# Attention ahead of two feed-forward layers: a pair's products with the values in two lumps instead of five parts

## The chip, the cores and the metric

The kernel runs on one core of a Trainium2 chip. The metric is the device time of one execution in microseconds (us). TensorE (PE) multiplies matrices, VectorE (DVE) and ScalarE (ACT) read its results, GpSimd (POOL) does small work beside them, and SyncE (SP) issues transfers.

## The reference

```python
def _attn_ref(q, k, v, tau):                      # 4 x 8 heads, 576 rows, 64 columns, float32
    scores = scale * np.matmul(q, k.transpose(0, 1, 3, 2))
    thresh = np.max(scores, axis=-1, keepdims=True) - tau
    scores = np.where(scores >= thresh, scores, -1000000000.0)
    scores = scores - np.max(scores, axis=-1, keepdims=True)
    attn = np.exp(scores)
    attn = attn / (np.sum(attn, axis=-1, keepdims=True) + 1e-09)
    return np.matmul(attn, v).astype(np.float32)

def reference(...):
    x = attn_out.transpose(0, 2, 1, 3).reshape(B * S, H * D)      # 2304 x 512
    x = _moe_ref(x, ...)      # sigmoid(x @ w_gate) * (x @ w_val) @ w_out, inner width 1536
    return _moe2_ref(x, ...)  # g(x @ w_in) @ w_out, inner width 2048
```

## The kernel before

The first quarter of the span is attention, the rest the two feed-forward layers. The change touches attention alone. It treats two heads at a time: 16 pairs `p`, each in five steps `u` = 0 to 4. Steps 0 to 3 take 128 rows of queries for both heads (`e` = 0, 1); step 4 takes the 64 rows that are left of each head together as one block of 128. The loop over `t` runs over all steps (`p, u = divmod(t, 5)`), and each turn of it issues work of several stages:

- `scores` (PE, L252, L248 in step 4): queries by keys of step t into `wa` (head 0) and `wb` (head 1);
- `turns` (PE, L295, L296): transposes of the weights of step t-2 into `wt` and `left`;
- `attend` (PE, L319): transposed weights by values into `av`. A round 0 takes the 256 rows of steps 0 and 1, a round 1 the 320 rows of steps 2 to 4; each has five blocks of 128 keys, and each block two matmuls, one a head. The table `rounds` says at which step, counted from the pair's first, which blocks of which round are done;
- `maxima` (DVE, L261): scaling out of `wa` and `wb` into an `s` of two buffers, with the row's extreme;
- `copies` (ACT, L301, L305): `wt` and `left` of step t-2 into `r`, `rl`;
- `exponents` (ACT, L273) of step t;
- `drain` (ACT, L329): `av` into `xall`, where a round ends;
- `masks` (DVE, L281): weights `p` of step t-1, then `lt` (POOL, L288), which `turns` needs for its last transpose;
- `background`: conversions of the feed-forward weights. In step 0 of pairs 1 to 12 three DVE operations (L155 to L169) stand between `maxima` and `masks`; in step 0 of pairs 13 to 15 splits of the first feed-forward operands stand there.

So each engine has a fixed order, written out by the loop: on PE scores of t, transposes of t-2, products with values; on DVE maxima of t, background, masks of t-1. Scores of t+1 overwrite what maxima of t read. A float32 matmul is two matmul instructions in the profile, a transpose one: a round of ten matmuls is 20 instructions there.

`load_v` loads a pair's values into one of three buffers `vs`, with four transfers on SP's queue, in step 4 two pairs ahead. SP's queue also carries queries and keys (`load`, step 2), the sums of a pair (`dr`, step 2 of the next pair) and their spread over partitions (`rb`, step 3).

Of the kernel before, what the change touches and what calls it, by code (L numbers as in the profile page):

```python
# [10 lines left out]
F32 = mybir.dt.float32  # L11
F32R = mybir.dt.float32r
U32 = mybir.dt.uint32
AF = mybir.ActivationFunctionType
# [15 lines left out]
def kernel(  # L30
# [17 lines left out]
    nc = tc.nc  # L48
# [3 lines left out]
    NP, _, S = q.shape  # L52
    D = v.shape[3]
# [4 lines left out]
    P = 128  # L58
    HS = S // 2
    nf, R = divmod(S, P)  # L60
# [48 lines left out]
    def run(*gens):  # L109
        for g in gens:  # L110
            for _ in g:
                pass
# [87 lines left out]
    def attention():  # L200
# [6 lines left out]
        left, av = (banks.tile([P, 512], F32, name=n) for n in ("left", "av"))  # L207
# [5 lines left out]
        per, pp = sb("per", 1), sb("pp", 2)  # L213
# [1 line left out]
        U = nf + 1  # L215
        N = NP * U
        NR = (2 * P, 2 * P + R)
        rt = [per.tile([P, 2, nf, n], F32, name=f"r_{i}") for i, n in enumerate(NR)]
        rl = [per.tile([P, n], F32, name=f"rl_{i}") for i, n in enumerate(NR)]
        vs = [per.tile([P, 2, nf + 1, D], F32, name=f"v_{i}") for i in range(3)]  # L220

        qk, st, pt, lts, drs = {}, {}, {}, {}, {}
# [7 lines left out]
        def load_v(p):  # L230

            t = vs[p % 3]
            for e in range(2):
                es = slice(e * R, e * R + R)
                nc.sync.dma_start(out=t[:, e, :nf], in_=v[p][:, e * (nf + 1) : e * (nf + 1) + nf])
                nc.sync.dma_start(out=t[es, e, nf], in_=v[p][es, nf])
# [6 lines left out]
        def scores(p, u):  # L243
            t = qk[p]
            for s in range(2):
                c = slice(s * HS, s * HS + HS)
                if u == nf:
                    nc.tensor.matmul(wa[:, s, :HS], corners[p % 2], t[:, 1, c], start=True, stop=True)  # L248
                    continue
                for e, w in enumerate((wa, wb)):  # L250
                    es = slice(e * D, e * D + D)
                    nc.tensor.matmul(  # L252
                        w[:, s, :HS], t[es, 0, u * P : u * P + P], t[es, 1, c], start=True, stop=True
                    )

        def maxima(p, u):

            t = sp.tile([P, 2, 2, HS], F32, tag="s", name="s")
            mx = mxs[(p * U + u) % 2]
            for e, w in enumerate((wa, wb)[: 1 if u == nf else 2]):  # L260
                nc.vector.tensor_scalar(  # L261
                    t[:, e], w[:, :, :HS], nscale, None, op0=ALU.mult, op1=ALU.min, accum_out=mx[:, 0, e : e + 1]
                )
                nc.gpsimd.tensor_scalar(
                    mx[:, 1, e : e + 1], mx[:, 0, e : e + 1], tau_b, None, op0=ALU.add
                )
            st[p, u] = t, mx

        def exponents(p, u):
            t, mx = st[p, u]  # L270
            ex = pe_.tile([P, 2, 2, HS], F32, tag="ex", name="ex")
            for e in range(1 if u == nf else 2):
                nc.scalar.activation(ex[:, e], t[:, e], AF.Exp, scale=-1.0, bias=mx[:, 0, e : e + 1])  # L273
            st[p, u] = t, mx, ex
# [15 lines left out]
        def turns(p, u):  # L290
            pr = pt.pop((p, u))
            for e in range(1 if u == nf else 2):
                for c in range(nf):
                    cs = slice(c * P, c * P + P)
                    nc.tensor.transpose(wt[:, e, cs], pr[:, e, cs], ident)  # L295
            nc.tensor.transpose(left[:, :P], lts.pop((p, u)).rearrange("p a b -> p (a b)"), ident)  # L296

        def copies(p, u):
            r, o = min(u // 2, 1), u % 2 * P if u < nf else 2 * P
            if u < nf:  # L300
                nc.scalar.activation(  # L301
                    rt[r].rearrange("p e c n -> p (e c) n")[:, :, o : o + P],
                    wt.rearrange("p e (c n) -> p (e c) n", n=P), AF.Copy,
                )
                nc.scalar.activation(rl[r][:, o : o + P], left[:, :P], AF.Copy)  # L305
                return
            for e in range(2):
                es = slice(e * R, e * R + R)
                x = wt[:, 0].rearrange("p (c n) -> p c n", n=P)
                nc.scalar.activation(rt[r][:, e, :, o : o + R], x[:, :, es], AF.Copy)  # L310
                nc.scalar.activation(rl[r][es, o : o + R], left[es, es], AF.Copy)

        def attend(p, r, cs):


            n = NR[r]
            for c in cs:
                for e in range(2):
                    nc.tensor.matmul(  # L319
                        av[e * D : e * D + D, :n], vs[p % 3][:, e, c], rt[r][:, e, c] if c < nf else rl[r],  # L320
                        start=c == 0, stop=c == nf,
                    )

# [4 lines left out]
        def drain(p, r):  # L328
            nc.scalar.activation(x_of(p)[:, r * NR[0] : r * NR[0] + NR[r]], av[:, : NR[r]], AF.Copy)  # L329

        def denom(p):
            rs = sums[p % 2]
            nc.vector.reciprocal(rs, rs)

        def sum_rows(p):

            n = 2 * nf + 1
            nc.scalar.activation(rows[p % 2][:n], left[:n, P : 2 * P], AF.Copy)
            drs[p] = dram.tile([n, P], F32, tag="dr", name="dr")
            nc.sync.dma_start(out=drs[p], in_=rows[p % 2][:n])  # L340
# [7 lines left out]
        def normalise(p, s):  # L348
            x, c = x_of(p), slice(s * HS, s * HS + HS)
            nc.gpsimd.tensor_tensor(x[:, c], x[:, c], rbs[:, p % 2 * S :][:, c], op=ALU.mult)  # L350
# [32 lines left out]
        corner(0)  # L383
        bg = background()

        rounds = {5: (0, 0, 2), 6: (0, 2, 5), 7: (1, 0, 2), 8: (1, 2, 4), 9: (1, 4, 5)}
        final = {5: (0, 0, 5), 7: (1, 0, 5)}
        parts = {}
        for p in range(NP):
            for i, (r, a, b) in (rounds if p + 1 < NP else final).items():  # L390
                parts.setdefault(p * U + i, []).append((p, r, range(a, b)))
        for t in range(N + 9):
            p, u = divmod(t, U)
            on = t < N
            mk = divmod(t - 1, U) if 1 <= t <= N else None
            at = divmod(t - 2, U) if 2 <= t <= N + 1 else None

            pd, ud = divmod(t - U, U)
            pd2, ud2 = divmod(t - 2 * U, U)
            if ud2 in (2, 3) and 0 <= pd2 < NP:  # L400
                normalise(pd2, ud2 - 2)
            if on:
                scores(p, u)
            if t == N + 1:
                yield t - N, True
            if at:
                turns(*at)
            if ud == 2 and 0 <= pd < NP:
                nc.tensor.transpose(left[: 2 * nf + 1, P : 2 * P], sums[pd % 2], ident)
            for part in parts.get(t, ()):  # L410
                attend(*part)
            if on:
                maxima(p, u)
            if at:
                copies(*at)
            if on:
                exponents(p, u)
            if ud == 1 and 0 <= pd < NP:
                denom(pd)
            if on and u == 0 and p > 0:  # L420
                if p < 13:
                    next(bg, None)
                else:
                    yield t - N, "gap"
            if ud == 2 and 0 <= pd < NP:
                sum_rows(pd)
            for part in parts.get(t, ()):
                if part[2][-1] == nf:
                    drain(*part[:2])
            if mk:  # L430
                masks(*mk)
                if mk[1] == nf:
                    nc.gpsimd.tensor_scalar(sums[mk[0] % 2], sums[mk[0] % 2], 1e-9, None, op0=ALU.add)
            if on:
                if u == 1 and p + 1 < NP:
                    corner(p + 1)
                if u == 2 and p + 2 < NP:
                    load(p + 2)
                if u == 4 and p + 2 < NP:
                    load_v(p + 2)  # L440
                if t == 1 or u == 2 and p % 2 == 0 and p < 12:
                    next(bg, None)
            if ud == 3 and 0 <= pd < NP:
                spread(pd)
            if t == N - 1:
                wides[:] = [wb, wa, wt]
            if t == N:
                run(bg)
                nc.scalar.activation(dummy, half, AF.Sigmoid)
                st1.close()  # L450
            if t == N + 2:
                st2.close()
                ps_o.close()
            yield t - N, False
# [497 lines left out]
```

## Time and profile before

| | |
|---|---|
| three runs, median (lowest to highest) | 1143.67 us (1143.54 to 1144.02) |
| profiled execution | 1143.82 us, span 1142.0 us |
| busy over the span | PE 97%, DVE 74%, ACT 54%, POOL 12% |

The span goes from the first to the last instruction; the execution's time has 1.82 us around it. A busy engine is one with an instruction in flight. Matmuls overlap, so PE's busy share says little by itself, and the chain of work (what released each piece) is the better guide.

### The profile page before, as it was taken

The page shows a single profiled execution, that of the slowest core. Times are in us where ns is not written, and L with a number is a line of the kernel's source. Part 1 is how long each engine was busy: PE and PEld are TensorE (multiplying, and loading weights), DVE is VectorE, ACT ScalarE, POOL GpSimd, SP SyncE. Part 2 cuts the span into 40 slices and gives each one's busy share as a digit, 9 for nine tenths or more (in the row PEclk, how much of TensorE's full clock was granted, in tenths as well). Part 3 has the DMA queues.
Part 4 walks back from the last instruction along what each step waited for, and adds up shares of the span by engine and source line. Part 5 has one row for each costly group of instructions (what it writes and reads, how often), then busy time and mean ns, then how long its engine had stood idle before and what let it go on. Part 6 is the DMA issues. An engine that isn't in the chain of part 4 may idle for free.

```text
span 1142.0 us, 17341 instructions
## 1 busy us (share of the span) xinstructions
PE 1109.9 (97%) x6372; PEld 944.5 (83%) x6372; DVE 849.0 (74%) x1484; ACT 620.9 (54%) x1048; POOL 138.1 (12%) x315
## 2 busy tenths in 40 slices
PE   8999999999799999999999999989999999999998
PEld 5555656556699999999999999988888888988887
DVE  6888888888499999767777762576677767676663
ACT  5777777787444344333344322366566655656553
POOL 3444544555100000000000000000000000000000
PEclk9999999999999999999999999999999999999999
DMA  4323233220665566455446524032312432143301
GB/s 131 88 76 89 78 81 78 62 71 21 212 205 177 176 199 231 168 183 178 154 161 212 176 78 162 19 111 86 133 67 104 156 121 97 72 161 114 111 20 55
DMA packets 65141, 139.09 MB, mean 122 GB/s; under 512 B 9616, under 2 KB 35872, under 8 KB 65056
## 3 DMA queue, kind: packets, MB, share of 16 engines
q1 hardware_dynamic: 64912, 137.98, 36.1%
q8 instruction: 50, 0.82, 0.3%
q14 instruction: 35, 0.29, 0.1%
q10 hardware_dynamic: 144, 0.00, 0.0%
HBM read 111.15 MB, written 26.81 MB: 121 GB/s over the span
## 4 chain that ended last, share of the span: by engine, by line
PE 85%; DVE 8%; ACT 3%; issue 2%; DMA 1%; SPq 0%; POOL 0%; DVEq 0%; POOLq 0%; ACTq 0%
PE y L743 15%; PE pu L610 14%; PE y L761 13%; PE pgv L486 8%; PE pgv L485 8%; PE pgv L487 8%; PE av L319 6%; PE w L295 5%; PE w L252 5%; DVE s L261 2%; PE w L248 2%; DVE p L281 1%; DVE high L165 1%; ACT sqs L619 1%; ACT sqs L620 1%
## 5 line engine op out<-in xcount | busy, mean ns | idle before, releaser
L485 PE MATMUL pgv<-xflat,win 128*128 128x384 f32 x560 | 188.5, 337 | 5.9 <-ACT act L541 3.8
L486 PE MATMUL pgv<-xflat,win 128*128 128x384 f32 x560 | 188.4, 336 | 0.1
L743 PE MATMUL y<-wout,hh 128*128 128x512 f32 x576 | 185.4, 397 | 3.0 <-ACT hh L628 3.0
L487 PE MATMUL pgv<-xflat,win 128*128 128x384 f32 x560 | 188.3, 336 | 0.0
L761 PE MATMUL y<-hh,wout 128*128 128x512 f32 (+1 forms) x576 | 146.7, 337 | 0.0
L261 DVE TENSOR_SCALAR_CACHE_REDUCE s<-w,nscale 128x576 f32<-128x576 f32 x144 | 112.7, 816 | 33.6 <-PE w L252 23.8
L743 PEld LDWEIGHTS y<-wout,hh 128*128 128x128 f32 x576 | 108.9, 189 | 28.0 <-ACT hh L628 3.3
L545 DVE TENSOR_TENSOR act<-pgv,act 128x384 f32<-128x384 f32 x70 | 38.9, 556 | 104.2 <-PE pgv L487 103.9
L743 PE MATMUL y<-wout,hl 128*128 128x512 f32 x288 | 114.3, 397 | 0.5 <-DVE hl L629 0.5
L485 PEld LDWEIGHTS pgv<-xflat,win 128*128 128x128 f32 x560 | 105.9, 189 | 7.9 <-ACT act L541 4.1
L281 DVE SCALAR_TENSOR_TENSOR p<-s,mx,ex 128x576 f32<-128x576 f32 x144 | 112.1, 812 | 0.5 <-POOL lt L288 0.5
L541 ACT ACTIVATE act<-pgv 128x384 f32<-128x384 f32 x70 | 34.2, 489 | 137.1 <-PE pgv L487 136.8
L273 ACT ACTIVATE ex<-s,mx 128x576 f32<-128x576 f32 x144 | 104.8, 775 | 7.2 <-DVE s L261 6.8
L486 PEld LDWEIGHTS pgv<-xflat,win 128*128 128x128 f32 x560 | 106.0, 189 | 2.0 <-DVE xflat L477 0.4
L761 PEld LDWEIGHTS y<-hh,wout 128*128 128x128 f32 x576 | 98.1, 188 | 11.3
L610 PE MATMUL pu<-xflat,win 128*128 128x384 f32 x576 | 105.1, 337 | 1.0 <-DVE sqs L689 0.7
L487 PEld LDWEIGHTS pgv<-xflat,win 128*128 128x128 f32 x560 | 106.0, 189 | 0.0
L546 ACT ACTIVATE hh<-act 128x384 fp32r<-128x384 f32 x72 | 38.0, 527 | 121.7 <-DVE act L545 121.3
L610 PEld LDWEIGHTS pu<-xflat,win 128*128 128x128 f32 x576 | 100.6, 188 | 2.4 <-DVE sqs L689 1.4
L295 PEld LDWEIGHTS w<-ident,p 128*128 128x128 f32 x576 | 62.8, 141 | 41.6 <-ACT ex L273 36.6
L761 PE MATMUL y<-hl,wout 128*128 128x512 f32 (+1 forms) x288 | 97.1, 337 | 0.0
L301 ACT ACTIVATE r<-w 128x1024 f32<-128x1024 f32 x64 | 65.7, 1026 | 49.7 <-PE w L295 49.6
(140 smaller groups left out, 1928.6 us busy)
## 6 DMA issues: line engine op xcount, KB each, us to landing
wmore<-saved SPq DMA_DIRECT2D x32, 512.0 KB
words<-in_moe_w_out_dram SPq DMA_DIRECT2D x26, 512.0 KB
tsum<-tsaved SPq DMA_DIRECT2D x24, 512.0 KB
wmore<-saved SPq DMA_DIRECT2D x15, 768.0 KB
words<-in_moe_w_in_dram SPq DMA_DIRECT2D x16, 512.0 KB
saved<-w SPq DMA_DIRECT2D x16, 512.0 KB
w<-saved SPq DMA_DIRECT2D x16, 512.0 KB
w<-saved SPq DMA_DIRECT2D x9, 768.0 KB
```

What stands on the lines that cost most here:

```text
L261: nc.vector.tensor_scalar(t[:, e], w[:, :, :HS], nscale, None, op0=ALU.mult, op1=ALU.min, accum_out=mx[:, 0, e : e + 1])
L273: nc.scalar.activation(ex[:, e], t[:, e], AF.Exp, scale=-1.0, bias=mx[:, 0, e : e + 1])
L281: nc.vector.scalar_tensor_tensor(pr[:, e], t[:, e].rearrange("p a b -> p (a b)"), mx[:, 1, e : e + 1], ex[:, e].rearrange("p a b -> p (a b ...
L295: nc.tensor.transpose(wt[:, e, cs], pr[:, e, cs], ident)
L301: nc.scalar.activation(rt[r].rearrange("p e c n -> p (e c) n")[:, :, o : o + P], wt.rearrange("p e (c n) -> p (e c) n", n=P), AF.Copy,)
L319: nc.tensor.matmul(av[e * D : e * D + D, :n], vs[p % 3][:, e, c], rt[r][:, e, c] if c < nf else rl[r], start=c == 0, stop=c == nf,)
L485: nc.tensor.matmul(ps, ih[:, i, kk], xh[:, kk, c], start=(kk == 0), stop=False)
L486: nc.tensor.matmul(ps, ih[:, i, kk], xl[:, kk, c], start=False, stop=False)
L487: nc.tensor.matmul(ps, il[:, i, kk], xh[:, kk, c], start=False, stop=(kk == KD - 1))
L610: nc.tensor.matmul(ps[bank], l[:, k], r[:, k], start=bool(new) and k == m == 0, stop=k == HK - 1 and m == 2, skip_group_check=True,)
L743: nc.tensor.matmul(y[b], l[:, ts_], r, start=first and m == 0, stop=last and m == 2)
L761: nc.tensor.matmul(at(y, a, b), l[:, ds_], r[:, c], start=new and m == 0, stop=last and m == 2, skip_group_check=True,)
```

## The change

Round 0 of a pair is done in one lump in step 1 of the next pair (`6`), round 1 in one lump in step 0 of the pair after that (`10`). Before, round 0 was split over steps 0 and 1 of the next pair, round 1 over its steps 2, 3 and 4. For the last pair but one, round 1 comes at step 4 of the last pair (`9`); the last pair keeps its two lumps. Since round 1 now outlives the next pair's `copies`, its `r` and `rl` exist twice, by `p % 2`. The values of pair p+1 are loaded in step 1 of pair p, where before those of pair p+2 were loaded in step 4.

```diff
-        rt = [per.tile([P, 2, nf, n], F32, name=f"r_{i}") for i, n in enumerate(NR)]
-        rl = [per.tile([P, n], F32, name=f"rl_{i}") for i, n in enumerate(NR)]
+        rt = [[per.tile([P, 2, nf, n], F32, name=f"r_{i}{j}") for j in range(i + 1)] for i, n in enumerate(NR)]
+        rl = [[per.tile([P, n], F32, name=f"rl_{i}{j}") for j in range(i + 1)] for i, n in enumerate(NR)]
...
         def copies(p, u):
             r, o = min(u // 2, 1), u % 2 * P if u < nf else 2 * P
+            ra, rb = (x[r][p % 2 * r] for x in (rt, rl))
...
-        rounds = {5: (0, 0, 2), 6: (0, 2, 5), 7: (1, 0, 2), 8: (1, 2, 4), 9: (1, 4, 5)}
-        final = {5: (0, 0, 5), 7: (1, 0, 5)}
+        rounds = {6: (0, 0, 5), 10: (1, 0, 5)}
+        final = {NP - 2: {6: (0, 0, 5), 9: (1, 0, 5)}, NP - 1: {5: (0, 0, 5), 7: (1, 0, 5)}}
         parts = {}
         for p in range(NP):
-            for i, (r, a, b) in (rounds if p + 1 < NP else final).items():
+            for i, (r, a, b) in final.get(p, rounds).items():
                 parts.setdefault(p * U + i, []).append((p, r, range(a, b)))
...
-                if u == 4 and p + 2 < NP:
-                    load_v(p + 2)
+                if u == 1 and 1 <= p < NP - 1:
+                    load_v(p + 1)
```

On PE, from the transposes in step 0 of pair 3 to the end of its step 1, before (`w_126` and `w_127` are `wa` and `wb`, `w_128` is `wt`):

```order
L295 MATMUL w_128<-ident,p 128x128 x8
L296 MATMUL left<-ident,lt 128x128
L319 MATMUL av<-r_160,v_166 64x256 x4
L252 MATMUL w_126<-qk 128x288
L252 MATMUL w_127<-qk 128x288
L252 MATMUL w_126<-qk 128x288
L252 MATMUL w_127<-qk 128x288
L295 MATMUL w_128<-ident,p 128x128 x4
L296 MATMUL left<-ident,lt 128x128
L319 MATMUL av<-r_160,v_166 64x256 x4
L319 MATMUL av<-rl_162,v_166 64x256 x2
```

The same place of the changed kernel, whose lines are two further down:

```order
L295 MATMUL w_128<-ident,p 128x128 x8
L296 MATMUL left<-ident,lt 128x128
L321 MATMUL av<-r_162,v_167 64x320 x8
L321 MATMUL av<-rl_165,v_167 64x320 x2
L252 MATMUL w_126<-qk 128x288
L252 MATMUL w_127<-qk 128x288
L252 MATMUL w_126<-qk 128x288
L252 MATMUL w_127<-qk 128x288
L295 MATMUL w_128<-ident,p 128x128 x4
L296 MATMUL left<-ident,lt 128x128
L321 MATMUL av<-r_160,v_168 64x256 x8
L321 MATMUL av<-rl_163,v_168 64x256 x2
```

Step 0 has ten matmuls of 320 columns (round 1 of two pairs back) where four of 256 stood, step 1 ten of 256 where six stood.

On PE, steps 3 and 4 of a pair, before:

```order
L295 MATMUL w_128<-ident,p 128x128 x8
L296 MATMUL left<-ident,lt 128x128
L319 MATMUL av<-r_161,v_166 64x320 x4
L248 MATMUL w_126<-qk,corner_75 128x288 x2
L295 MATMUL w_128<-ident,p 128x128 x8
L296 MATMUL left<-ident,lt 128x128
L319 MATMUL av<-rl_163,v_166 64x320 x2
```

And in the changed kernel:

```order
L295 MATMUL w_128<-ident,p 128x128 x8
L296 MATMUL left<-ident,lt 128x128
L248 MATMUL w_126<-qk,corner_75 128x288 x2
L295 MATMUL w_128<-ident,p 128x128 x8
L296 MATMUL left<-ident,lt 128x128
L252 MATMUL w_126<-qk 128x288
```

Between scores and scores nothing but transposes is left in steps 2, 3 and 4. DVE, ACT and POOL keep their order apart from the drain of round 1, which moves with its lump.

SP's queue over one pair, before:

```order
L340 DMA dr<-row_78 9x128
L226 DMA qk<-in_q_dram 128x576
L227 DMA qk<-in_k_dram 128x576
L346 DMA rb<-dr 128x1x512
L346 DMA rb<-dr 128x1x64
L235 DMA v_166<-in_v_dram 128x256
L236 DMA v_166<-in_v_dram 64x64
L235 DMA v_166<-in_v_dram 128x256
L236 DMA v_166<-in_v_dram 64x64
L129 DMA raw_87<-in_moe_w_gate_dram 128x4x256
```

And in the changed kernel:

```order
L342 DMA dr<-row_78 9x128
L226 DMA qk<-in_q_dram 128x576
L227 DMA qk<-in_k_dram 128x576
L348 DMA rb<-dr 128x1x512
L348 DMA rb<-dr 128x1x64
L129 DMA raw_87<-in_moe_w_gate_dram 128x4x256
L235 DMA v_168<-in_v_dram 128x256
L236 DMA v_168<-in_v_dram 64x64
L235 DMA v_168<-in_v_dram 128x256
L236 DMA v_168<-in_v_dram 64x64
```

The value loads stand in the same place between the spread and the next pair's sums; only a weight load has moved ahead of them.

## Rows read from the trace of the kernel before

**Rows 1.** Busy time by stretch: us, busy (instructions) by engine, PE clock, DMA share, GB/s

```profile
28.11:273.62 245.51, 233.61 (x1655) 145.40 (x1653) 216.55 (x559) 184.43 (x349) 117.16 (x265) 1.00 0.28 74
273.62:287.48 13.86, 13.54 (x99) 8.58 (x97) 10.42 (x29) 9.95 (x18) 6.87 (x15) 1.00 0.11 30
```

**Rows 2.** Chain that ended last, 97 to 116: start us, us, what

```profile
98.19 1.17 PE w L252 x8
...
100.61 1.23 PE av L319 x8
...
107.52 0.69 PE av L319 x4
108.21 1.22 PE w L252 x8
...
110.97 0.35 DVE high L161
...
112.68 0.83 DVE p L281 x2
...
113.65 0.63 PE w L295 x4
...
114.38 1.45 PE av L319 x12
```

**Rows 3.** Timeline of DVE in pair 0 and at the start of pair 1

```profile
13.24 0.82 DVE L261 TENSOR_SCALAR_CACHE_REDUCE s<-w,nscale 128x576 f32<-128x576 f32 x1
...
15.46 0.82 DVE L281 SCALAR_TENSOR_TENSOR p<-s,mx,ex 128x576 f32<-128x576 f32 x1
...
16.41 0.82 DVE L261 TENSOR_SCALAR_CACHE_REDUCE s<-w,nscale 128x576 f32<-128x576 f32 x1
...
19.58 0.82 DVE L261 TENSOR_SCALAR_CACHE_REDUCE s<-w,nscale 128x576 f32<-128x576 f32 x1
```

**Rows 4.** Timeline of PE over the same stretch

```profile
14.12 1.97 PE L252 MATMUL w<-qk 64*128 64x288 f32 x8
...
17.29 1.24 PE L248 MATMUL w<-qk,corner 128*128 128x288 f32 x4
...
20.00 0.27 PE L296 MATMUL left<-ident,lt 128*128 128x128 f32 x1
20.46 1.24 PE L252 MATMUL w<-qk 64*128 64x288 f32 x8 [0.19 <-DVE s L261]
...
22.77 1.08 PE L319 MATMUL av<-r,v 128*64 128x256 f32 x8
```

**Rows 5.** Timeline, one step's scores on PE and their first maximum on DVE

```profile
115.76 1.24 PE L252 MATMUL w<-qk 64*128 64x288 f32 x8
...
117.03 0.82 DVE L261 TENSOR_SCALAR_CACHE_REDUCE s<-w,nscale 128x576 f32<-128x576 f32 x1 [0.29 <-PE w L252]
```

**Rows 6.** Chain at the last pair's lump of round 0

```profile
284.02 1.09 PE w L295 x8
285.11 0.11 PE left L296
285.22 2.33 PE av L319 x20
```

**Rows 7.** Timeline of PE at the last pair's lump of round 1

```profile
294.61 2.37 PE L319 MATMUL av<-r,v 128*64 128x320 f32 x16
...
297.45 0.45 PE L485 MATMUL w<-xflat,win 128*128 128x384 f32 x1
```

**Rows 8.** Timeline, the first round 0 (pair 0, in step 1 of pair 1)

```profile
26.66 1.08 PE L319 MATMUL av<-r,v 128*64 128x256 f32 x8
```

**Rows 9.** Timeline of ACT after the last lump

```profile
297.57 0.44 ACT L329 ACTIVATE xall<-av 128x320 f32<-128x320 f32 x1 [2.59 <-PE av L319]
```

**Rows 10.** Timeline, a value load on SP's queue in step 4

```profile
105.63 3.44 SPq L235 DMA_DIRECT2D v<-in_v_dram  x1
```

**Rows 11.** Busy time by stretch, as rows 1: pair 0, and after attention

```profile
8.53:22.77 14.24, 13.12 (x73) 8.14 (x73) 12.87 (x35) 10.46 (x17) 6.05 (x15) 1.00 0.41 136
...
313.50:317.30 3.80, 3.77 (x13) 3.78 (x14) 3.17 (x4) 1.90 (x4) 0.00 (x0) 0.58 1.05 322
```

More of the change, by code (lines that the diff above doesn't have):

```diff
@@ L299, in copies @@
             r, o = min(u // 2, 1), u % 2 * P if u < nf else 2 * P
+            ra, rb = (x[r][p % 2 * r] for x in (rt, rl))
             if u < nf:
                 nc.scalar.activation(
-                    rt[r].rearrange("p e c n -> p (e c) n")[:, :, o : o + P],
+                    ra.rearrange("p e c n -> p (e c) n")[:, :, o : o + P],
                     wt.rearrange("p e (c n) -> p (e c) n", n=P), AF.Copy,
                 )
-                nc.scalar.activation(rl[r][:, o : o + P], left[:, :P], AF.Copy)
+                nc.scalar.activation(rb[:, o : o + P], left[:, :P], AF.Copy)
                 return
@@ L309, in copies @@
                 x = wt[:, 0].rearrange("p (c n) -> p c n", n=P)
-                nc.scalar.activation(rt[r][:, e, :, o : o + R], x[:, :, es], AF.Copy)
-                nc.scalar.activation(rl[r][es, o : o + R], left[es, es], AF.Copy)
+                nc.scalar.activation(ra[:, e, :, o : o + R], x[:, :, es], AF.Copy)
+                nc.scalar.activation(rb[es, o : o + R], left[es, es], AF.Copy)
         def attend(p, r, cs):
             n = NR[r]
+            ra, rb = (x[r][p % 2 * r] for x in (rt, rl))
             for c in cs:
@@ L319, in attend @@
                     nc.tensor.matmul(
-                        av[e * D : e * D + D, :n], vs[p % 3][:, e, c], rt[r][:, e, c] if c < nf else rl[r],
+                        av[e * D : e * D + D, :n], vs[p % 3][:, e, c], ra[:, e, c] if c < nf else rb,
                         start=c == 0, stop=c == nf,
```

## The prediction

> **What bounds the kernel now.** I first read the busy time by stretch. From the scores of step 2 of pair 1 to those of step 2 of pair 15 there are 14 pairs in 245.51 us [rows 1], 17.54 us a pair. PE is busy for 95% of it, DVE for 88%, so neither hides the other, and the order inside a pair decides. I write S0 to S4 for the start of the scores in steps 0 to 4.
>
> The chain of work over one pair is read next. From S2 at 98.19 to the next S0 at 108.21 it stays on PE: scores, transposes, products, scores again, 10.02 us without a gap [rows 2]. In step 0 it leaves PE for the background conversions on DVE, which begin after the two maxima and hold back the masks of the left-over rows until 112.68; their transposes start at 113.65, the 12 products of round 0 at 114.38, and these end 1.45 us later at the next S2 [rows 2]. That is 7.62 us, and 17.64 in all. So the pair has two stages: PE in steps 2 to 4, a detour over DVE in steps 0 and 1.
>
> What DVE needs by itself shows in pair 0, where no products stand on PE. There the first maxima of steps 2, 3 and 4 begin 3.17 us apart (13.24, 16.41, 19.58) [rows 3]: two maxima and two masks in a row. The second mask begins at 15.46, three operations in, so three steps of 0.74; from it to the next maximum there are 0.95 [rows 3]. I take the extra 0.21 for the `s` buffer, which that maximum rewrites and that mask has just read. Scores of the following step begin 0.88 after the first maximum (14.12, 17.29, 20.46) [rows 3, 4]; scores need 1.27 before their first maximum can start [rows 5].
>
> **The change part by part.** Steps 2 to 4 lose their products. PE then has scores and transposes alone there, and DVE's pace of 3.17 comes through. From S2: first maximum of step 2 at 1.27, of step 3 at 4.44, of step 4 at 7.61; scores of the next step 0 at 7.61 + 0.88 = 8.49. Before it was 10.02. PE has room: its scores and transposes fit, as pair 0 shows, where the same order kept the same 3.17. ACT is busy for 184 of 245 us [rows 1]; its copies and exponents of these steps are unchanged and also kept up in pair 0. They are counted at nothing; if they fell behind, the masks would wait for them.
>
> Step 0 gets the lump of round 1. Scores to the start of products take 2.31 (20.46 to 22.77) [rows 4], with the masks in the same position before S0 as here. The lump itself, 20 instructions of 320 columns, is there already in the last pair: 294.61 to the next matmul at 297.45, 2.84 us [rows 7]. S0 to S1 is 5.15. Under it lie DVE's two maxima, the conversions and one mask: the first of these maxima starts 10.04 after S2 (7.61, then one maximum and two masks at 0.74, then the gap of 0.21), so 1.55 after S0; two maxima take 1.48, the conversions some 1.8 (the chain shows them from 110.97 to 112.68 [rows 2]), the mask 0.82 [rows 3]: 5.6 after S0. Transposes of that mask are due at S1 + 1.17 = 6.32. The detour is hidden, with 0.7 us to spare; without that cover it would be paid as before.
>
> Step 1: scores 1.17 (as at 98.19, rows 2), four transposes and one more 0.70 (the eight and one before products take 1.14 after scores, less four at 0.11), then the lump of round 0, 20 instructions of 256 columns, 2.33 us [rows 6]. S1 to S2 is 4.20. The pair comes to 8.49 + 5.15 + 4.20 = 17.84 us against 17.54: **0.30 us more**, 4.2 us over 14 pairs.
>
> Why so near: what is won is the detour over DVE and the start of a group of products. The latter shows in 8 instructions at 1.23 and 4 at 0.69 [rows 2]: 0.135 an instruction and 0.15 for each start. Round 1 in three parts costs 1.23 + 1.23 + 0.69 = 3.15, in one lump 2.84. What is lost is that PE has nothing to do while DVE works through steps 2 to 4.
>
> The Trainium skill (page "TensorE: Matmul & The Clock Gate", section "The mechanism") says that a weight load overlaps running matmuls only when its row group differs. By that rule the lump would save nothing, since all these loads fill the same rows. Rows 6 and 7 have whole lumps without such a cost, so this trace does not agree, and the sum keeps 2.84 and 2.33. By the rule the pair would be some 0.4 us longer.
>
> The two ends. First, round 0 of pair 0 begins in step 1 of pair 1 at 26.66 [rows 8], held by the same masks; with 2.33 it ends at 28.99 in place of 28.11: +0.88. Second, from S2 of the last pair to the end of its first lump it was 13.86 us [rows 1]. Now S4 comes at 5.32 (4.44 + 0.88), the last transpose 2.71 later (17.29 to 20.00), products 0.20 after it (as 22.77 follows the transpose before it) [rows 4], so 8.23; the lump of round 1 of pair 14 ends at 11.07; transposes to products 1.20 (284.02 to 285.22) and 2.33 [rows 6] end at 14.60: +0.74.
>
> Behind that PE goes straight on, ACT waits for the last lump before it drains it [rows 9], and the splits of the feed-forward operands follow on ACT. So I carry the delay on in full. The transfers of the first feed-forward words may start a microsecond earlier against PE than now, since DVE ends earlier; nothing waits for them at that point in the chain, so I give nothing for it.
>
> The second set of `r` and `rl` costs no instruction. Moved loads: the four transfers of values wait on SP's queue for the lump of step 0 (buffer p+1 is that of p-2). Behind them are the next pair's sums, queries and keys and the spread. A value load waits there 3.44 us today as well, for the last part of round 1 [rows 10], and its data is needed ten steps later. I count 0; if it held the queue, the sums would be spread later, and normalising has a further four steps of room.
>
> Sum: 4.2 + 0.88 + 0.74 = **5.9 us**. The profiled execution took 1143.82 and its span 1142.0, so 1149.7; the median of the runs is 0.15 below the profiled one, so **1149.5 us**.
>
> **The rivals.**
> (a) The forecast: DVE paces steps 2 to 4. Chance 0.80, between 1147 and 1152: 0.05 us either way in the four parts of a pair gives 14 x 0.2 = 2.8.
> (b) It ends level. The 0.21 between mask and maximum is DVE's own and not the buffer's, or falls away when DVE comes in rested after the lumps. Two such gaps lie between S2 and S0, so 8.07 in place of 8.49: 0.42 x 14 = 5.9 us, just the whole loss; this is the point from which it decides. 1143.8. For it: DVE idles before S2. Against: all three steps of pair 0 show the gap. 0.08.
> (c) It ends faster. PE stays the bound, and steps 2 to 4 cost only PE's work: 2.41 (98.19 to 100.61), 2.30 (the same without the 0.11 for the sums), about 2.2 for the corner's step: 6.9 in place of 8.49. The pair is 16.2, 14 x -1.3 = -18.2, +1.6 at the ends: 1127. It needs maxima that run ahead of their scores; `wa` and `wb` are single, so it speaks against itself. With something between (b) and (c), 0.07.
> (d) Worse. The starts are not saved in the steady state: 14 x 0.44 = 6.2 more, 1155.7. Chance 0.03.
> (e) PE's clock drops in steps 2 to 4. Pair 0 has the same mixture of scores, transposes and gaps with the clock granted in full, 1.00, that is 2.4 GHz [rows 11]. Where PE had waited several microseconds after attention it fell to 0.58, nearly the lower level of 1.2 GHz [rows 11]. With PE's 6.9 us doubled, 13.8 in place of 8.49: 14 x 5.3 = 74, so 1224. Chance 0.02.
> The Trainium skill (same page, section "Part 4: PE-mode transpose") says that transposes do not count as a busy PE for this clock, which speaks for (e), as little else remains in these steps; pair 0's clock of 1.00 over 14 us of just that does not bear it out.
>
> **How the numbers follow.** The prediction is that of (a). A measurement of this kernel tells about 0.2% from no change, 2.3 us. (a), (d) and (e) are slower, 0.85, of which I move 0.01 to level for the lower end of (a); (b) and that are the same, 0.09; (c) is faster, 0.07. The range runs from 1145.5, between (a) and (b), to 1153, above (a) and short of (d): it leaves out (b) to (e), 0.20.
>
> **What would show it.** Right: 17.8 us from S2 to S2 in every pair, without the alternation by conversion; first maxima of steps 2, 3, 4 at 3.17 apart; PE idle about 1.6 us a pair, before transposes and before scores, released by DVE; lumps of 2.84 and 2.33; no wait for L169 before the left-over transposes. Wrong: first maxima less than 3 us apart (b, c); 20 products over 3.1 us (d); a clock below 1.00 before 290 us (e); masks waiting for ACT's exponents, or PE for values, in steps 0 to 2.

## The result, and the profile after

| | before | after |
|---|---|---|
| median of five runs (lowest to highest) | 1143.87 us (1143.54 to 1144.18) | 1149.50 us (1149.19 to 1151.78) |
| profiled execution | 1143.82 us | 1150.89 us |

The changed kernel is slower by a factor of 1.0055 (95% interval 1.004 to 1.007). The forecast was 1149.5, between 1145.5 and 1153.

Busy time by stretch of the changed kernel, over the same two stretches as [rows 1]; the columns are those of that group.

```profile
29.06:278.55 249.49, 242.07 (x1655) 152.47 (x1653) 216.23 (x559) 184.93 (x349) 117.34 (x264) 1.00 0.24 73
278.55:293.07 14.52, 14.17 (x99) 8.98 (x97) 9.64 (x27) 9.19 (x17) 6.28 (x14) 1.00 0.18 25
```

The 14 pairs took 245.51 us and take 249.49 now, 17.82 a pair against 17.54. PE's busy sum has grown with the span, though its work has not: a matmul that is issued and waits is busy too (in the next rows the scores of step 3, at 102.76, last 1.71 us, those of step 2 last 1.24).

The timeline of PE in the changed kernel over one pair (start us, us, instruction), from the scores of step 2 at 100.35 to those of the next step 2 at 118.17:

```profile
100.35 1.24 PE L252 MATMUL w<-qk 64*128 64x288 f32 x8
...
102.76 1.71 PE L252 MATMUL w<-qk 64*128 64x288 f32 x8
...
105.68 1.24 PE L248 MATMUL w<-qk,corner 128*128 128x288 f32 x4
107.24 1.31 PE L295 MATMUL w<-ident,p 128*128 128x128 f32 x8 [0.33 <-DVE p L281]
...
108.84 1.24 PE L252 MATMUL w<-qk 64*128 64x288 f32 x8 [0.19 <-DVE s L261]
...
111.15 2.38 PE L321 MATMUL av<-r,v 128*64 128x320 f32 x16
...
113.99 1.24 PE L252 MATMUL w<-qk 64*128 64x288 f32 x8
...
115.86 1.95 PE L321 MATMUL av<-r,v 128*64 128x256 f32 x16
...
118.17 1.24 PE L252 MATMUL w<-qk 64*128 64x288 f32 x8
```

S2 to S0 is 8.49 us, S0 to S1 5.15, S1 to S2 4.18. Where PE waits, DVE releases it. The lumps take 2.84 (111.15 to 113.99) and 2.31 (115.86 to 118.17).

The timeline of DVE over the same pair:

```profile
101.62 0.82 DVE L261 TENSOR_SCALAR_CACHE_REDUCE s<-w,nscale 128x576 f32<-128x576 f32 x1 [1.06 <-PE w L252]
...
103.84 0.82 DVE L281 SCALAR_TENSOR_TENSOR p<-s,mx,ex 128x576 f32<-128x576 f32 x1
...
104.79 0.82 DVE L261 TENSOR_SCALAR_CACHE_REDUCE s<-w,nscale 128x576 f32<-128x576 f32 x1
...
107.96 0.82 DVE L261 TENSOR_SCALAR_CACHE_REDUCE s<-w,nscale 128x576 f32<-128x576 f32 x1
...
113.08 0.69 DVE L169 TENSOR_TENSOR w<-w,high 128x512 f32<-128x512 f32 x1
113.69 0.81 DVE L281 SCALAR_TENSOR_TENSOR p<-s,mx,ex 128x576 f32<-128x576 f32 x1
```

The first maxima of steps 2, 3 and 4 begin 3.17 apart, as in pair 0 [rows 3], with 0.95 from the second mask to the next maximum. The conversions end under the lump, and the left-over mask behind them is done at 114.5, before its transposes are due at 115.16. The two kinds of pair that alternated before (17.64 and 17.37, by which three conversions fell in it) are now alike.

Attention ends (first product of the feed-forward layers on PE) at 293.07 after 287.48. The rest of the profiled execution took 1.5 us more than before, at a PE clock that differs there (last section).

### The profile page after: what moved, and what is told of

The parts are those of the page before. It is cut to its first block, busy times and chain, and to the rows that moved or that the text cites. A ratio compares the mean times of both kernels' runs of the same rounds, so it can differ in the third digit from the quotient of the medians.

```text
span 1149.1 us, 17344 instructions
## 1 busy us (share of the span) xinstructions
PE 1121.8 (98%) x6372; PEld 953.2 (83%) x6372; DVE 848.0 (74%) x1484; ACT 621.7 (54%) x1048; POOL 137.6 (12%) x315
## 3 DMA queue, kind: packets, MB, share of 16 engines
HBM read 111.15 MB, written 26.81 MB: 120 GB/s over the span
## 4 chain that ended last, share of the span: by engine, by line
PE 83%; DVE 8%; ACT 5%; issue 4%; DMA 0%; DVEq 0%; POOL 0%; SPq 0%; POOLq 0%; ACTq 0%
PE y L745 15%; PE pu L612 14%; PE y L763 13%; PE pgv L488 8%; PE pgv L487 8%; PE pgv L489 8%; PE av L321 7%; PE w L252 5%; PE w L295 4%; ACT ex L273 2%; DVE p L281 2%; DVE s L261 2%; ACT sqs L621 1%; ACT sqs L622 1%; ACT hh L630 1%
## 5 line engine op out<-in xcount | busy, mean ns | idle before, releaser
L252 PE MATMUL w<-qk 64*128 64x288 f32 x512 | 90.0, 432 | 4.1 <-DVE s L261 4.0
```

Of the source, the lines that this page charges most:

```text
L252: nc.tensor.matmul(w[:, s, :HS], t[es, 0, u * P : u * P + P], t[es, 1, c], start=True, stop=True)
```

## The experiments

Each was timed beside the kernel before, whose median was 1143.59 us beside e1 to e4 and 1143.56 beside the others. Profiled executions differ by up to 1.3 us in when attention begins, so attention is given from the scores of pair 0's step 4 to the first feed-forward product: 270.19 us before (17.29 to 287.48), 275.68 after (17.39 to 293.07).

**e1: the changed kernel with a third `s` buffer.**

```diff
-        qkp, sp, pe_ = sb1("qk", 3), sb1("sp", 2), sb1("pe_", 2)
+        qkp, sp, pe_ = sb1("qk", 3), sb1("sp", 3), sb1("pe_", 2)
```

> The changed kernel with three buffers for s in place of two. Theory: the 0.21 us between the last mask and the next first maximum is the wait for the s buffer that this mask has just read; with a third buffer the gap goes from 0.95 to 0.74, first maxima of steps 2, 3, 4 come 2.96 apart in place of 3.17, S2 to S0 takes 8.07 in place of 8.49, the pair 17.40, and the time falls by 14 x 0.42 = 5.9 to about 1143.6. Rival: the 0.21 belongs to DVE's change from masks to maxima itself; the gap stays at 0.95 and the time at 1149.5.

Measured: 1142.75 us (1140.83 to 1143.53, 10 runs), 0.999 of the kernel before (0.998 to 0.9999). Timeline of DVE in e1, one pair:

```profile
117.75 0.82 DVE L281 SCALAR_TENSOR_TENSOR p<-s,mx,ex 128x576 f32<-128x576 f32 x1
...
118.49 0.81 DVE L261 TENSOR_SCALAR_CACHE_REDUCE s<-w,nscale 128x576 f32<-128x576 f32 x1
...
121.45 0.81 DVE L261 TENSOR_SCALAR_CACHE_REDUCE s<-w,nscale 128x576 f32<-128x576 f32 x1
```

The gap is 0.74, first maxima are 2.96 apart, a pair takes 17.39 and attention 269.19. So the 0.21 is the buffer, and DVE's pace is what the lumps expose: 0.43 a pair off that pace takes the whole loss back.

**e2: the kernel before with the second `r` and `rl` and the moved loads alone** (the diff is against the changed kernel, whose rounds it puts back).

```diff
-        rounds = {6: (0, 0, 5), 10: (1, 0, 5)}
-        final = {NP - 2: {6: (0, 0, 5), 9: (1, 0, 5)}, NP - 1: {5: (0, 0, 5), 7: (1, 0, 5)}}
+        rounds = {5: (0, 0, 2), 6: (0, 2, 5), 7: (1, 0, 2), 8: (1, 2, 4), 9: (1, 4, 5)}
+        final = {NP - 1: {5: (0, 0, 5), 7: (1, 0, 5)}}
```

> The kernel before with the two lesser parts of the change alone: second r and rl for round 1, and values loaded one pair ahead in step 1; the products in five parts as before. Theory: neither is on the path, 1143.7 within 1 us. Rival: a part of the loss comes from the moved loads holding SP's queue or from the new places in memory; then over 1146.

Measured: 1143.41 us (1142.84 to 1144.98, 10 runs), 1.000 (0.9991 to 1.001); attention 270.16. These parts cost nothing that can be told.

**e3: the kernel before with the background work behind the masks.**

```diff
-            if on and u == 0 and p > 0:
-                if p < 13:
-                    next(bg, None)
-                else:
-                    yield t - N, "gap"
...
             if mk:
                 masks(*mk)
...
+            if on and u == 0 and p > 0:
+                if p < 13:
+                    next(bg, None)
+                else:
+                    yield t - N, "gap"
```

> The kernel before with one thing moved: the background work of step 0 stands behind the masks of the left-over rows on DVE, not ahead of them. Products in five parts as before. Theory: the detour over DVE in steps 0 and 1 is what PE waits for before; without it the transposes of the left-over rows start without a wait, the second maxima come some 0.7 us late for step 1 and cost a part of it, a pair takes about 16.9 in place of 17.54, and the time falls by 9 to 10, to about 1134. Rival: PE's own work sets the pair and the wait only moves to the next step; then 1143 to 1144.

Measured: 1133.99 us (1132.93 to 1136.11, 4 runs), 0.9918 (0.9903 to 0.9933); attention 261.37, pairs of 17.02 and 16.75. The chain of work in e3 from the products in step 0 to the scores of the next step 2 (start us, us, what):

```profile
106.84 1.01 PE av L319 x8
107.86 1.17 PE w L252 x8
109.03 0.59 PE w L295 x4
109.62 0.11 PE left L296
109.73 1.45 PE av L319 x12
111.17 1.54 PE w L252 x8
```

The left-over transposes follow the scores at once; before, the chain left PE here for 4 us [rows 2]. What is left of the detour is the 1.54 where scores take 1.17: their second half waits for the second maximum of step 1, which the conversions made late. Timeline of DVE at that maximum:

```profile
110.61 0.81 DVE L261 TENSOR_SCALAR_CACHE_REDUCE s<-w,nscale 128x576 f32<-128x576 f32 x1
```

**e4: the kernel before with all of round 0 in step 0.**

```diff
-        rounds = {5: (0, 0, 2), 6: (0, 2, 5), 7: (1, 0, 2), 8: (1, 2, 4), 9: (1, 4, 5)}
+        rounds = {5: (0, 0, 5), 7: (1, 0, 2), 8: (1, 2, 4), 9: (1, 4, 5)}
```

> The kernel before with round 0 in one lump in step 0 (not in step 1), round 1 in three parts in steps 2 to 4 as before. Theory: PE work put where DVE makes its detour hides the detour, and steps 2 to 4 keep their products, so that DVE does not pace them; step 0 is 4.64, step 1 1.87 on PE, the left-over transposes find their masks done; with masks of step 0 somewhat late in step 2 a pair takes 16.7 to 17.0, the first round ends 1.2 us earlier, and the time is 1131 to 1136. Rival: lumps as such are what costs (PE and DVE take turns), and a pair takes 17.5 or more; then 1143 or above.

Measured: 1142.82 us (1141.61 to 1145.3, 10 runs), 0.999 (0.9979 to 1.0001): the expectation failed, and the rival's 17.5 a pair came (17.51). Timeline of PE in e4, scores of steps 1, 2 and 3:

```profile
94.23 1.24 PE L252 MATMUL w<-qk 64*128 64x288 f32 x8
...
96.39 1.97 PE L252 MATMUL w<-qk 64*128 64x288 f32 x8 [0.21 <-DVE s L261]
...
100.76 0.51 PE L252 MATMUL w<-qk 64*128 64x288 f32 x2
```

The transposes did find their masks, but step 1 had no products. It lasted 2.16, which is the loop of scores to maximum (1.27) and maximum to the next scores (0.88), and those next scores were torn apart by the second maximum: 1.97 for 1.24. Timeline of DVE in e4, the second maximum of step 1:

```profile
96.25 0.81 DVE L261 TENSOR_SCALAR_CACHE_REDUCE s<-w,nscale 128x576 f32<-128x576 f32 x1
```

Step 2 so became 4.37 (96.39 to 100.76) where it was 3.64. I had counted step 1 at PE's 1.87 and left the loop out. Not lumps as such, but a step of scores and transposes alone is what costs: it was not shorter than this loop on the single `wa` and `wb`. That is read from the trace; no run gives `wa` and `wb` a second buffer.

**e5: the kernel before with the lump of round 0 alone.**

```diff
-        rounds = {5: (0, 0, 2), 6: (0, 2, 5), 7: (1, 0, 2), 8: (1, 2, 4), 9: (1, 4, 5)}
+        rounds = {6: (0, 0, 5), 7: (1, 0, 2), 8: (1, 2, 4), 9: (1, 4, 5)}
```

> The kernel before with one lump of the change alone: round 0 in step 1, round 1 in its three parts in steps 2 to 4 as before. Theory: step 0 keeps nothing but scores and transposes, so the conversions on DVE are not covered, and the larger lump stands behind the wait: S0 to S2 is 5.5 + 0.66 + 2.33 = 8.5 where it was 7.62, a pair about 18.4, and the time is 1155 to 1158. Rival: the lump of round 0 hides the detour, or the start that it saves shows; then 1143.7 or less.

Measured: 1162.06 us (1160.62 to 1165.04, 4 runs), 1.0161 (1.0142 to 1.018). In the profiled execution most pairs took 18.50 and 18.24, as expected; the remaining 4 to 5 us are three pairs in which PE's clock fell. The timeline of PE shows one of them:

```profile
192.56 0.80 PE L295 MATMUL w<-ident,p 128*128 128x128 f32 x4 [1.39 <-DVE p L281]
...
193.50 3.30 PE L319 MATMUL av<-r,v 128*64 128x256 f32 x16
...
197.16 1.24 PE L252 MATMUL w<-qk 64*128 64x288 f32 x8
```

The lump took 3.66 where 2.31 is usual. So a lump in step 1 does not hide the detour: it stands behind the transposes that wait. PE work in step 0 does hide it, be it round 1's lump, as in the changed kernel, or round 0's, as in e4.

**e6: the changed kernel with the background work behind the masks** (the edit of e3).

> The changed kernel with the background work of step 0 behind the masks of the left-over rows. Theory: in the changed kernel the lump of round 1 covers the conversions, so the same move that took 10 us from the kernel before gives nothing in the steady state (17.82 a pair), and about 1 us in the first pair, where no lump stands in step 0 yet: 1148 to 1149.5. Rival: the detour still costs in the changed kernel; then 1145 or less.

Measured: 1147.75 us (1145.21 to 1149.46, 10 runs), 1.0032 (1.0022 to 1.0042) of the kernel before. Timeline of PE in e6, two scores of step 2:

```profile
80.72 1.24 PE L252 MATMUL w<-qk 64*128 64x288 f32 x8
...
98.54 0.76 PE L252 MATMUL w<-qk 64*128 64x288 f32 x4
```

Still 17.82 a pair. Attention is 274.52, 1.16 less than in the changed kernel, which is the first pair. The median is a quarter of a microsecond below what was expected. The move that took 9.6 us from the kernel before takes 1.8 here (1149.50 to 1147.75), none of it in the steady state; the 0.6 beyond the first pair is not accounted for.

**e8: the kernel before with the conversions one at a time** behind the masks of steps 0, 3 and 4 of each pair (`load_w` before the sixth, the last).

```diff
-                run(itertools.islice(ops, 3))
-                yield
-                run(ops)
-                if g + 2 < 6:
-                    load_w(0, g + 2)
-                yield
+                for i, _ in enumerate(ops):
+                    if i == 5 and g + 2 < 6:
+                        load_w(0, g + 2)
+                    yield
...
-            if on and u == 0 and p > 0:
-                if p < 13:
-                    next(bg, None)
-                else:
-                    yield t - N, "gap"
...
+            if on and (u == 0 and 0 < p < 13 or u > 2 and p < 12):
+                next(bg, None)
+            if on and u == 0 and p > 12:
+                yield t - N, "gap"
```

> The kernel before, its conversions one operation at a time behind the masks of steps 0, 3 and 4 (three operations in step 0 before); products in five parts. Theory: behind the masks, three at once make the second maxima and then the masks of step 0 late, and 0.1 to 0.4 us of step 2 are still a wait; one at a time fits into DVE's slack of each step, PE's own work of 16.65 sets the pair, and the time is 1130 to 1132. Rival: the rest of the wait is not from the conversions; then 1134 as with all three behind the masks.

Measured: 1131.46 us (1130.21 to 1132.02, 4 runs), 0.9889 (0.9874 to 0.9903), faster than both kernels. Busy time by stretch over ten pairs of e8:

```profile
33.80:200.27 166.47, 166.47 (x1183) 103.86 (x1181) 151.91 (x403) 129.62 (x246) 99.20 (x191) 1.00 0.32 85
```

16.65 us a pair, all of it PE. It is the sum of its own work, as far as the trace shows: PE is never idle in it, and none of its scores lasts longer than 1.24, as they would if they waited. In the last three pairs, where the splits of the feed-forward operands stand together in step 0, step 1 is still up to 0.6 longer.

**e9: e8 with round 1 in two parts** (the diff shows this step alone; e8's edit is in it too).

```diff
-        rounds = {5: (0, 0, 2), 6: (0, 2, 5), 7: (1, 0, 2), 8: (1, 2, 4), 9: (1, 4, 5)}
+        rounds = {5: (0, 0, 2), 6: (0, 2, 5), 7: (1, 0, 2), 8: (1, 2, 5)}
```

> The kernel with conversions spread as before it in this call, and round 1 in two parts (two blocks in step 2, three in step 3) in place of three. Theory: one start of products less, 0.15 us a pair, and step 4 at 2.15 on PE is just as long as scores and the maximum that frees their buffer need (1.27 + 0.88): 2 us less than with three parts. Rival: step 4 without products falls behind that loop, and the pair is longer by a few tenths: 2 to 4 us more.

Measured: 1131.17 us (1131.14 to 1133.06, 4 runs), 0.9892 (0.9877 to 0.9906): neither, no difference from e8 that can be told. Step 4 is 2.16 as counted. Timeline of DVE in e9, the conversion behind the masks of step 4 and the maximum of step 0, whose scores began at 102.74:

```profile
104.08 0.70 DVE L165 SCALAR_TENSOR_TENSOR high<-raw,high 128x512 f32<-128x512 uint32 x1
104.68 0.82 DVE L261 TENSOR_SCALAR_CACHE_REDUCE s<-w,nscale 128x576 f32<-128x576 f32 x1
```

The maximum begins 1.94 after its scores where 1.27 would do. In such pairs step 0 takes 3.51 for 3.32, and pairs alternate between 16.77 and 16.50: the 0.15 saved is given back to DVE in every second pair.

## Why the prediction was right

**The pace of DVE in steps 2 to 4** was the step on which it stood: S2 to S0 at 8.49, measured 8.49. e1 shows that it is the cause and not an attendant: changing nothing but the buffer that sets the pace moved a pair from 17.82 to 17.39. That the 0.21 belongs to the `s` buffer was a guess in the prediction, and is shown by the same run: 0.95 became 0.74. Rival (b) was right about the price (a loss just undone) and wrong about the reason that it would come by itself.

**The hidden detour.** S0 to S1 5.15 as predicted, conversions under the lump with 0.7 us to spare. e3 and e6 together show it: the same move of the conversions is worth 9.6 us without the lump of round 1 and nothing a pair with it. e5 shows that the lump in step 1 alone hides nothing.

**The lumps** were 2.84 and 2.31 (2.33 was used), so the starts are saved in the steady state too and rival (d) is out. The Trainium skill's rule that a weight load overlaps running matmuls only with another row group ("TensorE: Matmul & The Clock Gate", section "The mechanism") does not fit these lumps either, whose 20 loads all fill the same rows: at 0.137 us each in the profile the loads alone add up to 2.74 us, more than the 2.31 of the shorter lump. The same section also lets a load go ahead that fills a background weight buffer; the prediction left that out, and the lumps do not speak against it.

**The balance of a pair.** e8 gives PE's own work with the products in five parts, for which the prediction had no row: 16.65. The five parts take 3.15 for round 1 and 2.46 for round 0 (1.01 and 1.45 in e3's chain), the lumps 5.15, which is 0.46 less, so 16.19 now, as rival (c) had it. Before, 0.89 of the 17.54 was a wait, the detour; now 1.63 of the 17.82 is one, for DVE. The change won 0.89 and 0.46 and lost 1.63. One sign was named wrongly: PE was to be idle some 1.6 a pair, and is idle for 0.53 (249.49 less 242.07, over 14 pairs). The rest of the wait stands in matmuls that are issued and count as busy.

**The sum.** 14 pairs gave 3.98 (4.2 predicted), the first pair 0.85 (0.88 predicted: 28.11 became 29.06, but 0.10 of that is attention beginning later in this execution), the end 0.66 (0.74: 13.86 became 14.52). That is 5.49 for attention against 5.9, each term a little under its forecast. The medians differ by 5.63, the profiled executions by 7.07, with 1.5 of it behind attention. So that the median fell on 1149.5 to the digit is luck; the pair and its parts are not. The loads and the second buffers were counted at nothing, and e2 bears that out. The scores of steps 3 and 0 waited for DVE's maxima (1.71 at 102.76, a wait of 0.19 at 108.84), so PE could not run ahead and (c) had no place.

**The clock**, rival (e), stayed at 1.00 in the attention of the changed kernel. It was not as idle a thought as its 0.02 suggests: e5 met it, though in steps 0 and 1.

## What to carry to other kernels

When two engines take turns, moving work of one into a few steps pays only if the steps that it leaves are not paced by the other: find a stretch of the trace where that work is absent (here pair 0) and read the pace there. Before moving the big work to cover a wait, look at what stands ahead in the queue of the engine that is waited for; putting three small conversions behind the masks, and then apart, gave 12 us where covering them cost 6. A step that is stripped of its filling falls back on its shortest loop (scores, maximum, scores on a single buffer, 2.15 us here), which no count of either engine's work shows.

## What the runs showed of the hardware that was not expected

PE's clock fell in e5 inside attention, in three of its pairs. Busy time by stretch, the lump in one of them:

```profile
193.50:196.63 3.13, 3.13 (x17) 1.85 (x18) 2.15 (x7) 2.31 (x6) 1.84 (x6) 0.56 0.03 5
```

The granted clock was 0.56, close to the lower level of 1.2 GHz, and the lump cost about 1.35 us more. PE had waited 1.39 us ahead of it, between scores and a few transposes. The timeline of PE four pairs earlier, in the same step, shows the same wait without a fall:

```profile
119.09 0.63 PE L295 MATMUL w<-ident,p 128*128 128x128 f32 x4 [1.39 <-DVE p L281]
```

So the same wait has it one time and not another; what decides was not settled. The other two falls came after waits of 1.12 and 1.33 us. The Trainium skill ("TensorE: Matmul & The Clock Gate", section "Part 4: PE-mode transpose"), by which transposes do not count as a busy PE, would fit a fall after steps of scores and transposes, but no run here takes the transposes apart from the wait, and steps 2 to 4 of the changed kernel, of just scores and transposes, stayed at 1.00.

Behind attention PE waits longer, 3.76 us in the kernel before and 3.80 in the changed one, and there the fall differs between the two profiled executions. Busy time by stretch over the same work, from a product just ahead of this wait to one some 18 us later, the changed kernel first:

```profile
309.08:328.02 18.94, 12.82 (x52) 11.29 (x51) 18.05 (x21) 7.16 (x13) 2.53 (x2) 0.73 0.53 191
```

and the kernel before:

```profile
303.46:321.46 18.00, 12.14 (x51) 10.94 (x51) 17.15 (x20) 7.18 (x13) 3.21 (x2) 0.81 0.51 175
```

With the lower clock the same work took 0.94 us longer, most of the 1.5 us behind attention. The runs of the changed kernel with a mean clock of 0.994 took 1149.2 to 1149.5, those of 0.993 and 0.991 took 1150.9 and 1151.8. So that part of the spread, up to 2.6 us, goes with the clock. Whether the change has a hand in it, five runs do not show.
